# Interleaving the first expert's products with the second expert's search, two more clock-holding matmuls, and other PSUM banks for the last attention unit

## Chip, cores and metric

One NeuronCore of a Trainium2 chip. The metric is the device time of one execution in microseconds (us). All of a run's executions are listed with their mean granted TensorE clock (1 is full speed). With one core there is no second die to compare with, so a run counts as slow only if it is more than 1.5% above the fastest one of its kernel.

Engines: PE is TensorE, PEld its weight loads, DVE VectorE, ACT ScalarE, POOL GpSimd, SP the engine that issues most transfers. L1310 is a line of the kernel.

## Reference

Two blocks. A linear attention (RWKV-5) over 4 batches, 8 heads, 768 steps, and behind it a balanced mixture of 8 experts, in which each of 3072 tokens goes to one expert and each expert takes 384 of them:

```python
logits = x @ w_gate                       # x: (3072, 384), the attention's output
order = np.argsort(-logits.flatten())     # greedy: best (token, expert) pairs first
for idx in order:
    tok, e = int(idx) // E, int(idx) % E
    if assigned[tok] >= 0 or counts[e] >= cap:
        continue
    assigned[tok] = e; counts[e] += 1
...
for e in range(E):
    mask = assigned == e
    h = np.maximum(x[mask] @ w1[e], 0.0)  # 384 x 1024
    out[mask] = h @ w2[e]                 # 1024 x 384
```

## The kernel before

The kernel doesn't sort. It finds which expert fills up first and at which logit (the "search": three rounds of counting tokens above 16 thresholds), lists that expert's tokens, gathers their rows, computes that expert, strikes them out, and goes on. While TensorE computes one expert, VectorE searches for the next. A count of the search is three small matmuls, then VectorE, then one matmul that sums; a hook `between` lets other TensorE work stand between these.

```python
class Assignment:
    MEANWHILE = 2, 3, 5
    between = staticmethod(lambda n: None)
    behind = None

    def count(self, pool, m, prop, cand, digit_of):
        ...
        self.asked = tt(ind, self.by_token(m, ND), self.by_expert(cand), ALU.is_ge)   # DVE
        ...
        for j in range(NT // G):
            nc.tensor.matmul(each..., ind[...], prop[...], ...)                       # "counts", x3
        self.between(self.MEANWHILE[0])
        ...                                                                           # DVE: own, cnt, wide
        nc.tensor.matmul(all_ps..., self.ones_h, wide..., start=True, stop=True)      # the sum
        self.between(self.MEANWHILE[1])
        return all_ps

    def likely(self, fmax, acc, place, flag):
        ...
        for g in range(3):
            with ExitStack() as order:
                if self.behind is not None:
                    order.enter_context(self.tc.issue_after(self.behind))   # search behind this product
                    self.behind = None
                all_ps = self.count(pool, m, prop, cand, self.digit_of)
            ...

    def settle(self, out, ask, fetch, asked=False):
        fetch(out["tok"])                    # three indirect gathers of 128 rows
        if not asked:
            ask(out["fmax"])                 # weights of that expert
        ...
        with self.tc.If(found < 1):          # a rare path, a branch on every engine
            ...
        self.leave(out["fmax"], out["acc"])
```

The last unit of the attention and its logits (`y_ps` is one tile for all units; `turned` holds x):

```python
    def from_state(n):
        ...
                nc.tensor.matmul(y_ps[halves[i], j, g, :], state[b][heads[j], a, :], ...)
    def outputs(n):
        ...
        nc.scalar.copy(turned[n].rearrange("p (g j) t -> p j g t", j=2), y_ps[:, :, 0:2, :])
    def logits(c):
        ...
        for a in range(HP):
            for b in range(B):               # the four batches in four 32-partition strips
                nc.tensor.matmul(lg_ps[ts(b, 32), 0, :], wg_sb[:, a, :], xTs[b][:, a, :], ...)
```

The first expert's opening and the loop over experts:

```python
    def opening(hid, at):
        xT = xpool.tile([128, KD, CAP], F32, name="xT")
        h_pss = [...]                        # four PSUM tiles, one for each of four hidden columns
        turn_rows(xT, at["xg"], 0)           # transposes of the first 128 gathered rows, copied by ACT
        for c in range(NC):
            for j, h_ps in enumerate(h_pss):
                product = products(h_ps, j, at["w1"], xT, ts(c, 128))   # three 128-column matmuls
                if j == 1 and c + 1 < NC:
                    with tc.issue_after(product):
                        copied = turn_rows(xT, at["xg"], c + 1)
                    ...
        walk.behind = product                # the next search behind ALL of them
        ...

    awake = ps_t.tile([128, KD, 128], F32, name="xT_ps")
    for _ in range(4):                       # "warming": keeps TensorE busy while the rows come
        nc.tensor.matmul(awake, ident, ident.unsqueeze(1).to_broadcast([128, KD, 128]), start=True, stop=True)
    walk.settle(ahead, ask_half, fetch(xg), asked=True)
    for n in range(E):
        ...
        if n == 0:
            xT = opening(hid, at)
            done = KF // 2
        else:
            walk.behind = hidden(hid, 0, at["w1"], xT)
        if n + 1 < E:
            ahead = following(n + 2 == E)    # search, settle, weights of the next expert
        for j in range(done, KF):
            hidden(hid, j, at["w1"], xT)
        for c in range(NC):
            if c == NC - 1 and n + 1 < E:
                xT = turn(ahead["xg"])
            result(n, c, hid, at["w2"], at["tok"])
```

## Time and profile before

| | before |
|---|---|
| median of 3 runs | 425.59 us (424.44 to 425.62) |
| profiled run, its span | 425.35 us, 423.6 us |
| first products of the first expert | 142.02 us |
| first count of the second expert's search | 152.46 us |
| second expert's list ready | 167.88 us |
| TensorE waits for the second expert's rows | 4.67 us, to 176.73 us |
| first products of the second expert | 184.74 us |
| from there to the end | 238.9 us |

### The profile page before, as it was taken

What the parts mean: (1) busy time and instruction counts of PE and PEld (TensorE: products, weight loads), DVE (VectorE), ACT (ScalarE), POOL (GpSimd) and SP (SyncE); (2) the same over time, 40 slices, a digit from 0 to 9 for tenths busy, and PEclk for the clock granted to TensorE, in tenths of its full rate; (3) what the DMA queues carried; (4) which work ended last, traced back from release to release, by engine and by line L of the source; (5) the groups of instructions that cost most, each with busy time, mean ns of one, the idle gap of its engine ahead of it and who ended that gap; (6) DMA issues with size and microseconds to landing.
All of it is one profiled execution on the core that took longest, in us unless ns stands there. A gap on an engine that the chain in (4) does not pass through costs nothing. (4 is left out here: it accounts for less than half of the span.)

```text
span 423.6 us, 7986 instructions
## 1 busy us (share of the span) xinstructions
PE 401.4 (95%) x2978; PEld 266.5 (63%) x2978; DVE 198.4 (47%) x656; ACT 153.6 (36%) x390; POOL 113.4 (27%) x154
## 2 busy tenths in 40 slices
PE   7899999999987899599999999999999999999993
PEld 4688888888775775355565565565555555565551
DVE  5898889997565247127318407505704703000000
ACT  3897877878564031112022122112121221211200
POOL 5566775466001101300310310210220030211011
PEclk9999999999999899899999999999999999999999
DMA  9999999910068353702810820740550496201001
GB/s 148 164 164 188 173 179 157 185 22 4 2 215 306 86 203 135 259 19 61 313 37 7 305 82 19 235 158 19 171 221 20 149 350 207 60 19 39 0 19 37
DMA packets 93994, 54.39 MB, mean 128 GB/s; under 512 B 76785, under 2 KB 88177, under 8 KB 93937
## 3 DMA queue, kind: packets, MB, share of 16 engines
q1 hardware_dynamic: 89280, 41.70, 40.0%
q0 software_dynamic: 3072, 9.44, 6.4%
q10 hardware_dynamic: 1584, 2.56, 1.8%
q8 instruction: 27, 0.44, 0.4%
q14 instruction: 31, 0.25, 0.2%
HBM read 44.25 MB, written 9.44 MB: 127 GB/s over the span
## 5 line engine op out<-in xcount | busy, mean ns | idle before, releaser
L1289 PE MATMUL h_ps<-xT,w 128*128 128x384 f32 (+1 forms) x396 | 130.5, 479 | 0.7 <-DVE low L952 0.7
L1323 PE MATMUL o_ps<-w,hid 128*128 128x384 f32 x384 | 130.4, 491 | 0.7
L1323 PEld LDWEIGHTS o_ps<-w,hid 128*128 128x128 f32 x384 | 71.1, 191 | 47.4 <-issue 3.9
L1289 PEld LDWEIGHTS h_ps<-xT,w 128*128 128x128 f32 x396 | 69.8, 193 | 39.7 <-issue 3.8
L1296 ACT ACTIVATE hid<-h_ps 128x384 f32<-128x384 f32 x60 | 29.5, 492 | 94.0 <-PE h_ps L1289 84.2
L1326 POOL DMA_INDIRECT out_dram<-o_sb,tok x24 | 23.6, 985 | 142.3 <-ACT o_sb L1325 114.3
L453 ACT ACTIVATE AT<-ident,dd 128x128 f32<-128x128 f32 x192 | 59.6, 396 | 1.5 <-DVE dd L448 1.5
L1219 POOL DMA_INDIRECT xg<-x_rows,tok x24 | 23.6, 982 | 124.6 <-issue 101.2
L1325 ACT COPY o_sb<-o_ps 128x384 f32<-128x384 f32 x24 | 11.5, 480 | 111.5 <-PE o_ps L1323 111.5
L871 DVE TENSOR_TENSOR own<-counts,same 128x64 f32<-128x64 f32 x21 | 4.7, 225 | 89.6 <-PE counts L883 89.6
L522 DVE COPY_PREDICATED AT<-mask,g_ps 128x512 f32<-128x512 uint8 x48 | 32.5, 730 | 7.1 <-PE g_ps L520 7.1
L520 PE MATMUL g_ps<-rT,kT 48*128 48x128 f32 x384 | 28.4, 285 | 0.1
L445 POOL TENSOR_TENSOR rk<-rk,u_bc 128x384 f32<-128x384 f32 x24 | 27.3, 1135 | 1.9
L444 POOL TENSOR_TENSOR rk<-rt,kt 128x384 f32<-128x384 f32 x24 | 24.8, 1034 | 8.2 <-DMA rt<-in_r_dram 3.7
L520 PEld LDWEIGHTS g_ps<-rT,kT 48*128 48x128 f32 x384 | 23.6, 187 | 4.9 <-issue 2.9
L555 PE MATMUL y_ps<-AT,vt 128*64 128x128 f32 x384 | 25.7, 276 | 0.0
L555 PEld LDWEIGHTS y_ps<-AT,vt 128*64 128x64 f32 x384 | 20.6, 137 | 1.1 <-issue 0.3
L1279 ACT COPY xT<-xT_ps 128x384 f32<-128x384 f32 x24 | 11.0, 485 | 24.1 <-PE xT_ps L1278 14.8
L434 DVE TENSOR_TENSOR ks<-kt,wk 128x384 f32<-128x384 f32 x24 | 19.4, 808 | 0.0
L465 DVE TENSOR_TENSOR rT<-rT_ps,wr 128x512 f32<-128x512 f32 x24 | 16.4, 684 | 5.3 <-PE rT_ps L460 5.2
L1278 PE MATMUL xT_ps<-ident,xg 128*128 128x128 f32 x72 | 12.1, 294 | 5.8 <-DMA xg<-x_rows,tok 5.8
L473 ACT COPY kT<-kT_ps 128x512 f32<-128x512 f32 x24 | 14.1, 586 | 8.9 <-PE kT_ps L471 8.6
(203 smaller groups left out, 404.1 us busy)
## 6 DMA issues: line engine op xcount, KB each, us to landing
w<-in_moe_w_dram SPq DMA_DIRECT2D x14, 1536.0 KB, 10.5
kt<-in_k_dram SPq DMA_DIRECT2D x24, 192.0 KB, 4.5
rt<-in_r_dram SPq DMA_DIRECT2D x24, 192.0 KB, 5.1
vt<-in_v_dram SPq DMA_DIRECT2D x24, 192.0 KB, 4.8
x_rows<-AT SPq DMA_DIRECT2D x8, 192.0 KB, 2.7
w<-in_moe_w_dram ACTq DMA_DIRECT2D x1, 1536.0 KB
x_rows<-rt SPq DMA_DIRECT2D x6, 192.0 KB, 1.9
x_rows<-ks SPq DMA_DIRECT2D x5, 192.0 KB, 2.2
```

Source lines behind the costliest of these rows:

```text
L434: self.tc.nc.vector.tensor_mul(self.live[n]["ks"][:, :, 0:D], self.live[n]["kt"], self.wk.rearrange("p (h d) -> p h d", h=H))
L444: nc.gpsimd.tensor_mul(rk, rt[:, :, 0:D], kt)
L445: nc.gpsimd.tensor_mul(rk, rk, self.u_bc.rearrange("p (h d) -> p h d", h=H))
L453: self.tc.nc.scalar.activation(AT[:, h % 2, h // 2, :], self.ident, AF.Copy, scale=dd[:, h:h + 1])
L520: nc.tensor.matmul(g_pss[q][:, a, :], kT[heads[q], a, :], rT[heads[q], a, :], start=True, stop=True)
L522: nc.vector.copy_predicated(out=AT[:, q], mask=mask.unsqueeze(1).to_broadcast([128, HP, T]), data=g_pss[q])
L555: nc.tensor.matmul(y_ps[halves[i], j, g, :], vt[:, 2 * a + j, :], AT[:, j, a, :], start=(c == 0 and g == 0), stop=(g == 1), skip_group_che ...
L1219: nc.gpsimd.indirect_dma_start(out=xg[:, c, :], out_offset=None, in_=x_dram, in_offset=bass.IndirectOffsetOnAxis(ap=tok[:, c:c + 1], axis=0))
L1289: product = nc.tensor.matmul(h_ps[:, cols], w1[:, f, ts(j, 128)], xT[:, f, cols], start=(f == 0), stop=(f == KD - 1))
L1296: nc.scalar.activation(hid[:, j, :], h_ps, AF.Relu)
L1323: nc.tensor.matmul(o_ps, hid[:, j, ts(c, 128)], w2[:, j, :], start=(j == 0), stop=(j == KF - 1))
L1326: nc.gpsimd.indirect_dma_start(out=out_rows[n * NC + c], out_offset=bass.IndirectOffsetOnAxis(ap=tok[:, c:c + 1], axis=0), in_=o_sb, in_of ...
```

## The change

The intent: (1) the last unit writes its y to two other PSUM banks, so that it need not wait for the copy of the unit before; (2) one more warming matmul ahead of the first expert's transposes and one behind them, so that the clock stays full; (3) the opening becomes a generator, and the search for the second expert pulls its pieces through `between`, so the search runs inside the first expert's products instead of behind them.

```diff
+    def banks_of(n):
+        if n < N - 1:
+            return [y_ps[:, j] for j in range(2)]
+        if not last:
+            last.extend(mild.ps.tile([128, HP, T], F32, name=f"y_{tag}", tag=tag) for tag in ("kT_ps", "rT_ps"))
+        return last
 ...
-        nc.scalar.copy(turned[n].rearrange("p (g j) t -> p j g t", j=2), y_ps[:, :, 0:2, :])
+        into = turned[n].rearrange("p (g j) t -> p j g t", j=2)
+        if n < N - 1:
+            nc.scalar.copy(into, y_ps[:, :, 0:2, :])
+        else:
+            nc.scalar.copy(into[:, 0], y[0][:, 0:2, :])
+            nc.vector.tensor_copy(into[:, 1], y[1][:, 0:2, :])
 ...
-        for a in range(HP):
-            for b in range(B):
-                nc.tensor.matmul(lg_ps[ts(b, 32), 0, :], wg_sb[:, a, :], xTs[b][:, a, :], ...)
+        for some in ((range(B),) if c < C - 1 else (range(B - 1), (B - 1,))):
+            for a in range(HP):
+                for b in some:
+                    nc.tensor.matmul(lg_ps[ts(b, 32), 0, :], wg_sb[:, a, :], xTs[b][:, a, :], ...)
 ...
+            if pieces:
+                def between(most):
+                    for _ in range(most):
+                        next(pieces, None)
+                with tc.manual_schedule(engines={nc.tensor.engine}):
+                    next(pieces)
+                    walk.between = between
+                    walk.search(at)
+                    walk.between = Assignment.between
+                    for _ in pieces:
+                        pass
 ...
-    def opening(hid, at):
+    def opening(hid, at, xT):
         turn_rows(xT, at["xg"], 0)
+        nc.tensor.matmul(ps_t.tile([128, KD, 128], F32, name="xT_ps"), ident,
+                         ident.unsqueeze(1).to_broadcast([128, KD, 128]), start=True, stop=True)
 ...
-        walk.behind = product
+                if c > 0 or j > 1:
+                    yield
+        for j in range(len(h_pss), KF):
+            h_ps = ps_h.tile([128, CAP], F32, name="h_ps")
+            for f in range(KD):
+                nc.tensor.matmul(h_ps, at["w1"][:, f, ts(j, 128)], xT[:, f, :], ...)
+                if f < KD - 1:
+                    yield
+            nc.scalar.activation(hid[:, j, :], h_ps, AF.Relu)
+            yield
 ...
-    for _ in range(4):
+    for _ in range(5):
         nc.tensor.matmul(awake, ident, ident.unsqueeze(1).to_broadcast([128, KD, 128]), start=True, stop=True)
```

More of the change, by code (lines that the diff above doesn't have):

```diff
@@ L512, in attention_mild @@
     g_pss = [ps.tile([128, HP, T], F32, name=f"g_ps{i}") for i in range(2)]
+    last = []
     order = [(g, j, i) for g in range(2) for j in range(2) for i in range(2)]
@@ L522, in pairs @@
             nc.vector.copy_predicated(out=AT[:, q], mask=mask.unsqueeze(1).to_broadcast([128, HP, T]), data=g_pss[q])
+    def banks_of(n):
[4 more added lines that the diff above has]
+        return last
     def from_state(n):
         b, c = units[n]
+        y = banks_of(n)
         if c > 0:
@@ L528, in from_state @@
                 a = 2 * g + i
-                nc.tensor.matmul(y_ps[halves[i], j, g, :], state[b][heads[j], a, :],
+                nc.tensor.matmul(y[j][halves[i], g, :], state[b][heads[j], a, :],
                                  live[n]["rT"][heads[j], a, :], start=(g == 0), stop=False, skip_group_check=True)
@@ L552, in outputs @@
         vt, AT = (live[n][x] for x in ("vt", "AT"))
+        y = banks_of(n)
         for g, j, i in order:
             a = 2 * g + i
-            nc.tensor.matmul(y_ps[halves[i], j, g, :], vt[:, 2 * a + j, :], AT[:, j, a, :],
+            nc.tensor.matmul(y[j][halves[i], g, :], vt[:, 2 * a + j, :], AT[:, j, a, :],
                              start=(c == 0 and g == 0), stop=(g == 1), skip_group_check=True)
-        nc.scalar.copy(turned[n].rearrange("p (g j) t -> p j g t", j=2), y_ps[:, :, 0:2, :])
+        into = turned[n].rearrange("p (g j) t -> p j g t", j=2)
[4 more added lines that the diff above has]
+            nc.vector.tensor_copy(into[:, 1], y[1][:, 0:2, :])
     def logits(c):
@@ L562, in logits @@
         lg_ps = ps.tile([128, 2, 128], F32, name="lg_ps")
-        for a in range(HP):
-            for b in range(B):
-                nc.tensor.matmul(lg_ps[ts(b, 32), 0, :], wg_sb[:, a, :], xTs[b][:, a, :],
-                                 start=(a == 0), stop=(a == HP - 1), skip_group_check=True)
+        for some in ((range(B),) if c < C - 1 else (range(B - 1), (B - 1,))):
+            for a in range(HP):
+                for b in some:
+                    nc.tensor.matmul(lg_ps[ts(b, 32), 0, :], wg_sb[:, a, :], xTs[b][:, a, :],
+                                     start=(a == 0), stop=(a == HP - 1), skip_group_check=True)
         by_e = pool.tile([128, 128], F32, name="lgT")
@@ L1261, in second, with following @@
         queue.dma_start(w2, moe_w2[which(at["number"], queue)].rearrange("o (c p) d -> p (o c) d", p=128))
-    def following(last):
+    def following(last, pieces=None):
         at = dict(walk.slots(), number=xpool.tile([1, 1], I32, name="number"),
@@ L1269, in following @@
         else:
-            walk.search(at)
+            if pieces:
[9 more added lines that the diff above has]
+                        pass
+            else:
+                walk.search(at)
             walk.settle(*make)
@@ L1297, in hidden @@
         return product
-    def opening(hid, at):
-        xT = xpool.tile([128, KD, CAP], F32, name="xT")
+    def opening(hid, at, xT):
         h_pss = [pool.tile([128, CAP], F32, name=name) for pool, name in ((ps_h, "h_ps"), (ps_o, "o_ps")) for _ in range(2)]
         turn_rows(xT, at["xg"], 0)
+        nc.tensor.matmul(ps_t.tile([128, KD, 128], F32, name="xT_ps"), ident,
+                         ident.unsqueeze(1).to_broadcast([128, KD, 128]), start=True, stop=True)
         for c in range(NC):
             for j, h_ps in enumerate(h_pss):
-                product = products(h_ps, j, at["w1"], xT, ts(c, 128))
+                products(h_ps, j, at["w1"], xT, ts(c, 128))
+                if c == NC - 1:
+                    nc.scalar.activation(hid[:, j, :], h_ps, AF.Relu)
                 if j == 1 and c + 1 < NC:
-                    with tc.issue_after(product):
-                        copied = turn_rows(xT, at["xg"], c + 1)
+                    copied = turn_rows(xT, at["xg"], c + 1)
                     if c + 1 == NC - 2:
@@ L1314, in opening @@
                             second(at, nc.scalar)
-        walk.behind = product
-        for j, h_ps in enumerate(h_pss):
+                if c > 0 or j > 1:
[3 more added lines that the diff above has]
+            for f in range(KD):
+                nc.tensor.matmul(h_ps, at["w1"][:, f, ts(j, 128)], xT[:, f, :], start=(f == 0), stop=(f == KD - 1))
+                if f < KD - 1:
+                    yield
             nc.scalar.activation(hid[:, j, :], h_ps, AF.Relu)
-        return xT
+            yield
     def result(n, c, hid, w2, tok):
@@ L1337, in rwkv5_eagle_then_base_layer_balanced @@
         hid = hpool.tile([128, KF, CAP], F32, name="hid")
-        done = 1
         if n == 0:
-            xT = opening(hid, at)
-            done = KF // 2
+            xT = xpool.tile([128, KD, CAP], F32, name="xT")
+            pieces = opening(hid, at, xT)
         else:
+            pieces = None
             walk.behind = hidden(hid, 0, at["w1"], xT)
         if n + 1 < E:
-            ahead = following(n + 2 == E)
-        for j in range(done, KF):
-            hidden(hid, j, at["w1"], xT)
+            ahead = following(n + 2 == E, pieces)
+        if n > 0:
+            for j in range(1, KF):
+                hidden(hid, j, at["w1"], xT)
         for c in range(NC):
```

## The prediction

> **What bounds the kernel now.** I read the page first, then the chain of waits, then the order of time on TensorE around the places that the change touches, then busy time and granted clock in short stretches. The page's slices say that TensorE (row PE) is full nearly everywhere, and where it is not:
>
> ```profile
> PE   7899999999987899599999999999999999999993
> PEclk9999999999999899899999999999999999999999
> ```
>
> One slice is 10.6 us. PE has a dip in slices 11 to 13 (the end of the attention part and the search for the first expert) and one in slice 16, at 169 to 180 us; the granted clock dips in slice 13 and slice 16. Everywhere else PE has 9, so a microsecond won outside those dips is won nowhere, and one won in them moves everything behind them. After 180 us PE is the bound to the end: in the table by stretches it is busy 114.55 of the 115 us from 185 to 300 and 115.70 of the 116 us from 300 to 416. So the end moves by as much as the first products of the second expert move (184.74 us in the timeline).
>
> The waits of TensorE, longest first, name the gap:
>
> ```profile
> PE xT_ps L1278 <- DMA xg<-x_rows,tok: 5.8, 3, 4.7
> ...
> PE h_ps L1289 <- DVE low L952: 0.7, 1, 0.7
> ```
>
> The timeline of TensorE over the first expert (start, us, what, idle before):
>
> ```profile
> 137.03 2.82 PE L1333 MATMUL xT_ps<-ident 128*128 128x384 f32 x8 [0.73 <-PE g_ps L658]
> 140.79 0.55 PE L1278 MATMUL xT_ps<-ident,xg 128*128 128x128 f32 x3 [0.94 <-DMA xg<-x_rows,tok]
> 142.02 2.57 PE L1289 MATMUL h_ps<-xT,w 128*128 128x128 f32 x12 [0.69 <-DVE low L952]
> ...
> 151.12 1.50 PE L1289 MATMUL o_ps<-xT,w 128*128 128x128 f32 x12
> 152.46 0.25 PE L883 MATMUL counts<-prop,ind 128*128 128x64 bf16 x3
> ...
> 167.31 4.76 PE L1323 MATMUL o_ps<-w,hid 128*128 128x384 f32 x14
> 176.73 0.87 PE L1278 MATMUL xT_ps<-ident,xg 128*128 128x128 f32 x3 [4.67 <-DMA xg<-x_rows,tok]
> ```
>
> To be seen: the second expert's search starts on TensorE only at 152.46, after all of the first expert's 128-column products. VectorE had its operand long before:
>
> ```profile
> 142.63 0.55 DVE L871 TENSOR_TENSOR ind<-m,cand 128x384 bf16<-128x384 f32 x1
> ...
> 152.74 0.22 DVE L871 TENSOR_TENSOR own<-counts,same 128x64 f32<-128x64 f32 x1 [9.29 <-PE counts L883]
> ```
>
> So the search sits 9.3 us behind products that it doesn't need. Its list (tok) is done at 167.88, the gather of the rows is issued at 169.22, 170.52 and 171.78 behind an output scatter, the rows land up to 7.2 us after issue beside 3 MB of weights, and TensorE has nothing from 172.05 to 176.73. Each pause is paid twice, for the clock falls after it (columns: stretch, PE, PEld, DVE, ACT, POOL busy, granted clock, DMA share, GB/s):
>
> ```profile
> 142.00:144.00 2.00, 1.98 (x11) 1.98 (x12) 1.42 (x4) 0.00 (x0) 0.00 (x0) 0.61 0.00 0
> 144.00:146.00 2.00, 2.00 (x12) 2.00 (x12) 0.00 (x0) 0.48 (x1) 0.00 (x0) 0.54 0.00 0
> ...
> 176.00:178.00 2.00, 1.05 (x4) 0.69 (x5) 0.00 (x0) 0.36 (x1) 0.00 (x0) 0.64 0.68 248
> 178.00:180.00 2.00, 2.00 (x6) 1.29 (x6) 0.00 (x0) 0.60 (x2) 0.00 (x0) 0.50 0.08 29
> ```
>
> In quarter microseconds the clock is 0.5 from about 142.4 to 145.8 and from 176.7 to 180.0.
>
> [...]two halved stretches of 3.4 and 3.3 us, whose starts lie 34.2 us apart, ten windows. [...]the window ahead of 142.45 holds 0.82 + 0.55 + 0.43 = 1.8 us of matmuls, 53%. [...]the data of y_ps must be copied before they are overwritten; so TensorE waits for ScalarE there (0.36 us, part 1 below), and another bank removes that wait.
>
> **The change, part by part.** The order of instructions shows that nothing else moves.
>
> *1. Last unit's x in other banks.* Now the state products of the last unit start at 114.31 after a wait of 0.36 us for the copy of the unit before. With other banks they follow the matmul before them, which ends about 113.9: 0.4 us. The copy falls into two halves, ScalarE and VectorE, beside each other; by the rows (0.59 us for 512 columns, 0.48 for 384) a half of 256 takes about 0.37, 0.2 us less, but TensorE has transposes (0.66) and the other twelve logit products in that time, so that gains nothing. VectorE's small operations on the guess (0.9 us) now stand behind its half copy and still end before 118. The logits, the search (bound by VectorE from 118 to 134), the list and the gather should all come 0.4 earlier: first transposes at 140.4 instead of 140.79. **-0.4 us.**
>
> *2. Fifth warming matmul, and one more behind the first transposes.* One is two records of 0.35, 0.7 us. Five run from 136.6 to 140.15, still ahead of 140.4. The sixth lies in the 0.69 us in which TensorE waits for the copy of the first transposes (ScalarE 0.48 us plus hand-overs). Both lie in idle time, cost 0.03 us, and make the window busy to about nine tenths. Then the clock stays full: 3.4 us at half clock did 1.7 us of work. **-1.7 us.**
>
> *3. Pieces between the counts.* Work on TensorE doesn't change. A 128-column product is two records of 0.112 us (six in 1.34), a 384-column one two of 0.333 (0.667). Before, 142.02 to 172.05 is 30.03 us, less 1.7 lost to the clock: 28.3 of work. In the new order, from a first product at 141.6: six products, three transposes, three products, and the first counts at about 143.95. Their operand is ready at 143.18 - 0.4. From there, with VectorE's steps as they are measured now (counts to wide 1.13 us, summed counts to the next ind 1.8, to acc 2.04, st_ps to vals 2.94, some_ps to part 0.83):
> - sum at 145.4 (wide ready at 145.1), second counts at 147.75 (ind at 147.2), sum at 149.3 (148.9), third counts at 151.4 (151.1), sum at 152.9 (152.5), st_ps at 154.95 (acc 154.9), some_ps at 158.4 (157.9), list at 159.2 (159.2), tok at 159.8 instead of 167.88.
>
> No step waits more than a tenth; the margins are those with which the later experts run without a wait, since six 128-column products take just what two 384-column ones take. The second half of w1 and w2 are issued behind the second copy, some 2 us earlier than 145.76; the stream's first 0.79 MB at 385 GB/s should be there by 148, and is needed at 150.7.
>
> The gather now stands ahead of the scatter on GpSimd: rows asked for at 159.85, 161.1 and 162.4. With the 7.2 us of the worst landing now, the first rows are there by 167.1 and the last by 169.6. TensorE has one hidden product and fifteen output products after the list, 16 x 0.667 = 10.7 us, to about 169.9. So the gather is covered, by some 2 us for the first rows, and no pause is left. Before, from 172.05 to the next expert's products at 184.74 is 12.7 us; the same work (nine transposes and eight output products) takes an expert later 6.3 us, from 212.32 on. The difference is 4.9 us of idle time and 1.5 of half clock. **-6.4 us.**
>
> *Sum.* 0.4 + 1.7 + 6.4 = 8.5 us: second expert's first products at 176.2, and everything behind as it is. The profiled run took 425.35, which gives 416.85. I add 0.35 us for small waits and for runs in which a window still falls badly: **417.2 us**, a ratio of 1.019 to 1.020. That is just about the 2% line.
>
> **Rivals.**
> - *The pause only moves (weights instead of rows).* The second expert's w1 is asked for at about 156 now instead of 164, beside nothing, and needs some 6 us; w2 follows at 161. Both are there before 170. For it: they share the queues with the gather, which took 7.2 us to land where three transfers met. If the rows landed 10 us after issue, 1 us would come back: 418.3.
> - *The search becomes the bound.* If VectorE took longer for a step than now, TensorE would wait at each of three sums and three counts, in fixed order. Margins are 0 to 0.6 us; 0.2 at each of the eight waits is 1.6, but the gather still has 2 us to spare, and waits on TensorE add to the end directly: 418.5.
> - *The clock still falls at the start.* If [...]the window falls badly, 1.7 us come back: 418.6. Against it: 0.25 us of idle time is left in 5 us.
> - *The branch, not the gather, sets 140.79.* TensorE and VectorE go on within 0.02 us of each other there, which speaks for it. If the branch waits for the warming matmuls, the fifth costs 0.7 us: 417.6. That TensorE crosses later such branches in a row of output products without a gap speaks against it.
> - *It gains more.* The three runs before spread from 424.44 to 425.62, as the phase of the windows would do. If the new kernel loses nothing and the first part gives 0.5, 416.3.
>
> **Range and chances.** The mechanism (search earlier by 8 us, pause of 4.7 us gone) I hold for 95% sure; what is open is some tenths. 416.2 to 419.0 holds 8 in 10. The 2% line is at 417.1 against the median of before, at 416.8 against their mean; my value is just above. Chances: 0.40 faster, 0.59 within, 0.01 slower.
>
> **What the profile would show.** Step 1: last unit's state products without the wait, first transposes at 140.4. Step 2: clock 1.00 from 140 to 148, and no gap over 0.3 us between the warming matmuls and the products. Step 3: first counts at 144, tok near 160, the wait of the transposes for xg near zero, clock 1.00 from 165 to 180, second expert's first products at 176.2. Wrong, if TensorE shows waits on VectorE inside the search, if the rows land after 170, or if half clock is still there after 140.

## The result, and the profile after

The changed kernel took 417.52 us (median of 4 runs, 417.33 to 418.27), the kernel before 425.08 us (4 runs, 424.44 to 425.62). The ratio is 0.9826, 95% interval 0.9804 to 0.9848, so the sign is sure and the 2% line is inside the interval. A ratio here is the mean time of one kernel's fast runs over that of the other's of the same rounds, so not quite the ratio of the medians. (The prediction writes its ratio the other way round: its 1.019 to 1.020 is 0.980 to 0.981 here.) On a second chip the same pair gave 0.9841 (0.9814 to 0.9867), 416.87 us against 424.48 us.

Start-up differs by some tenths from run to run (a matmul near 113 us, `most_ps`, which the change doesn't touch, starts at 113.47 us in the profile before and at 112.3 to 114.1 us in the others). Below, "M+" is a time from that matmul on; it takes this noise out.

The page's slices of the profile after (busy share of TensorE and granted clock, 40 slices of 10.4 us): the dip near 170 us is gone in both rows, and only the dip of the attention's end is left.

```profile
PE   7899999999987899999999999999999999999993
PEclk9999999999999999999999999999999999999998
```

The timeline of TensorE after the change (start, us, what, idle before):

```profile
137.15 3.46 PE L1373 MATMUL xT_ps<-ident 128*128 128x384 f32 x10 [0.86 <-PE g_ps L676]
140.92 0.52 PE L1310 MATMUL xT_ps<-ident,xg 128*128 128x128 f32 x3 [0.30 <-DMA xg<-x_rows,tok]
141.27 0.81 PE L1335 MATMUL xT_ps<-ident 128*128 128x384 f32 x2
142.13 1.60 PE L1321 MATMUL h_ps<-xT,w 128*128 128x128 f32 x12
...
144.56 0.25 PE L901 MATMUL counts<-prop,ind 128*128 128x64 bf16 x3
...
159.93 0.18 PE L1176 MATMUL list_ps<-part,alike 128*128 128x12 f16 x1
...
170.76 0.82 PE L1310 MATMUL xT_ps<-ident,xg 128*128 128x128 f32 x6
...
176.90 2.10 PE L1321 MATMUL h_ps<-xT,w 128*128 128x384 f32 x6
```

The first count stands at 144.56 instead of 152.46 us, the list's matmul at 159.93 instead of 167.27 (the list itself is done at 160.54 instead of 167.88), and the second expert's transposes at 170.76 follow the matmul before them with no wait in brackets. In the page of waits, the entry that headed the list before (5.8 us, three times) is down to the one wait of the first expert:

```profile
PE xT_ps L1310 <- DMA xg<-x_rows,tok: 0.3, 1, 0.3
```

The clock in two stretches, before and then after (stretch, PE, PEld, DVE, ACT, POOL busy with counts, granted clock, DMA share, GB/s):

```profile
142.00:148.00 6.00, 5.98 (x39) 5.98 (x40) 1.42 (x4) 0.48 (x1) 0.00 (x0) 0.72 0.10 19
...
172.00:180.00 8.00, 3.12 (x10) 1.97 (x10) 0.00 (x0) 1.44 (x3) 1.72 (x2) 0.79 0.71 260
```

```profile
142.00:148.00 6.00, 5.96 (x55) 5.85 (x55) 3.56 (x13) 1.03 (x3) 0.00 (x0) 1.00 0.32 100
172.00:180.00 8.00, 8.00 (x31) 4.80 (x31) 0.80 (x4) 1.65 (x4) 1.66 (x2) 1.00 0.13 49
```

Both stretches are at full clock now. The first is busy in both kernels, yet does 39 matmul records before and 55 after (the kernel before, when its clock stays full, does 55 too: see part 2 below): busy time alone doesn't show a halved clock, the count does.

From M to the second expert's first products it is 71.27 us before (184.74 - 113.47) and 63.28 us after (176.90 - 113.62): 7.99 us. From there to the end it is 238.9 us in both. The profiled runs differ by 425.35 - 417.49 = 7.86 us; the rest is start-up noise. So the whole gain is made between 113 and 185 us.

### The profile page after: what moved, and what is told of

Same layout as the page of the kernel before. It is cut to its first block, busy times and chain, and to the rows that moved or that the text cites. A ratio compares the mean times of both kernels' runs of the same rounds, so it can differ in the third digit from the quotient of the medians.

```text
span 415.8 us, 7996 instructions
## 1 busy us (share of the span) xinstructions
PE 400.0 (96%) x2982; PEld 265.3 (64%) x2982; DVE 198.8 (48%) x657; ACT 152.9 (37%) x390; POOL 112.8 (27%) x154
## 5 line engine op out<-in xcount | busy, mean ns | idle before, releaser
L1321 PE MATMUL h_ps<-xT,w 128*128 128x384 f32 (+1 forms) x372 | 121.1, 475 | 0.0
L1321 PEld LDWEIGHTS h_ps<-xT,w 128*128 128x128 f32 x372 | 64.8, 190 | 37.1 <-issue 3.4
L1328 ACT ACTIVATE hid<-h_ps 128x384 f32<-128x384 f32 x56 | 27.5, 491 | 87.5 <-PE h_ps L1321 77.7
L566 PE MATMUL y_ps<-AT,vt 128*64 128x128 f32 x368 | 24.6, 276 | 0.0
L566 PEld LDWEIGHTS y_ps<-AT,vt 128*64 128x64 f32 x368 | 19.7, 137 | 0.9 <-issue 0.3
L460 PE MATMUL rT_ps<-ident,rt 128*128 128x128 f32 x96 | 16.1, 292 | 1.1 <-DVE rT L465 1.1
(218 smaller groups left out, 418.4 us busy)
```

The lines of the kernel that those rows point to most:

```text
L566: nc.tensor.matmul(y[j][halves[i], g, :], vt[:, 2 * a + j, :], AT[:, j, a, :], start=(c == 0 and g == 0), stop=(g == 1), skip_group_check= ...
L1321: product = nc.tensor.matmul(h_ps[:, cols], w1[:, f, ts(j, 128)], xT[:, f, cols], start=(f == 0), stop=(f == KD - 1))
L1328: nc.scalar.activation(hid[:, j, :], h_ps, AF.Relu)
```

## The experiments

Twelve experiments ran, two of them the same kernels as in the result and one a repeat; eight on one chip (runs of the kernel before beside them: 424.17 us median of 12, 422.64 to 426.59, mean 424.20) and four on another (the kernel before, one run: 422.64). In the diffs, "-" is the changed kernel.

| run | median us (range, n) | ratio to before [95%] | mean us |
|---|---|---|---|
| change again | 416.87 (416.75 to 417.91, 5) | 0.9841 [0.9814, 0.9867] | 417.17 |
| banks undone | 417.10 (416.30 to 417.68, 5) | 0.9841 [0.9815, 0.9867] | 417.08 |
| no added warming | 417.57 (415.89 to 418.90, 6) | 0.9859 [0.9832, 0.9885] | 417.65 |
| old order of the logits | 416.68 (416.01 to 417.80, 5) | 0.9823 [0.9797, 0.9849] | 416.75 |
| no pieces (parts 1 and 2 alone) | 423.98 (422.77 to 425.29, 6) | 0.9998 [0.9971, 1.0025] | 424.09 |
| pieces alone (part 3 alone) | 418.59 (416.96 to 419.62, 6) | 0.9867 [0.9837, 0.9897] | 418.37 |
| rows sooner | 417.37 (415.89 to 418.03, 5) | 0.9839 [0.9809, 0.9869] | 417.20 |

The theory: nearly all comes from part 3, by taking away the wait for the second expert's rows and the half clock behind it. Rivals: the pause only moves; the first parts carry a good share; the branch, not the gather, sets the first expert's start.

### Which part carries it

*The change once more*, as the base of the comparisons on this chip.

> The change as it is, run again so that its parts can be compared on one chip. Both theories: 417.3 to 418.0 us, ratio to before 0.980 to 0.985, clock 1.00 from 140 to 180 us in the profile, no wait of the transposes for xg at the second expert.

Measured: 416.87 us, M to second expert's products 63.25 us. It repeats.

*Part 3 taken away*: the opening and the loop as before, with parts 1 and 2 kept.

```diff
-    def following(last, pieces=None):
+    def following(last):
 ...
-            if pieces:
-                ...
+            walk.search(at)
 ...
-    def opening(hid, at, xT):
+    def opening(hid, at):
 ...
+        walk.behind = product
```

> The kernel before with the change's first and second part, but with the first expert's products all ahead of the search, as before. Theory (the pieces carry most of the gain, 6.4 us as predicted): first counts some 10 us after the first product, the transposes wait some 4.7 us for xg, the clock falls to 0.5 after that wait but not after the warming matmuls; 1 to 1.7 us faster than before, ratio 0.996 to 0.998. Rival (the clock at the start is the main thing): 3 us or more faster than before and the wait shrinks.

Measured: ratio 0.9998, no gain to be seen (the interval ends at 0.9971, so the expected 0.996 isn't in it and 0.998 is). In its timeline the wait for the rows is back:

```profile
175.64 1.58 PE L1296 MATMUL xT_ps<-ident,xg 128*128 128x128 f32 x6 [4.76 <-DMA xg<-x_rows,tok]
```

The stretches around its end (columns as above) have a low clock for longer than in the profile before:

```profile
172.00:180.00 8.00, 4.36 (x13) 3.08 (x14) 0.00 (x0) 1.44 (x3) 0.81 (x1) 0.62 0.56 205
180.00:185.00 5.00, 5.00 (x15) 2.81 (x14) 0.00 (x0) 0.44 (x1) 0.00 (x0) 0.92 0.00 0
```

The clock was full in its opening (1.00 from 142 to 148 us), as part 2 intends, but in this execution the lost clock at the pause is 8 x 0.38 + 5 x 0.08 = 3.4 us, against 8 x 0.21 = 1.7 in the profile before. Of this, half of the 1.7 us from 173.94 to 175.64 falls into the wait itself, where it costs nothing. At the list this profile is 1.4 us ahead of the profile before (M+52.36 against M+53.80), at the second expert's products 0.6 us (M+70.64 against M+71.27): more than half of what part 2 saved at 142 us was lost again at the pause. Over six runs parts 1 and 2 alone are worth 424.20 - 424.09 = 0.1 us.

*Part 3 alone*: the banks, the order of the logits and the warming matmuls as before.

```diff
-        if n < N - 1:            # banks_of and outputs
+        if n < N:
-        for some in ((range(B),) if c < C - 1 else (range(B - 1), (B - 1,))):
+        for some in (range(B),):
-        nc.tensor.matmul(ps_t.tile([128, KD, 128], F32, name="xT_ps"), ident, ...)
-    for _ in range(5):
+    for _ in range(4):
```

> The change with its first and second part both undone, the pieces alone. Theory: the wait for xg is gone, so 5.5 to 7 us faster than before, ratio 0.983 to 0.987; executions with the clock at 0.5 after the first transposes take up to 1.7 us longer, so the runs spread more than those of the change. Rival (parts add up only together, since a slow clock at the start delays the search and brings the wait back): 4 us or less faster than before.

Measured: by the means 424.20 - 418.37 = 5.8 us. Put on top of parts 1 and 2, part 3 is worth 424.09 - 417.17 = 6.9 us; the whole change 7.0 us here (7.4 on the first chip). Part 3 alone carries five sixths of it. By the means the other parts are worth more with it (1.2 us) than without it (0.1 us), but runs of one kernel spread by 1 to 4 us, so that difference isn't shown.

### Part 1: the other banks

*Banks and logits as before, the rest as changed.*

```diff
-        if n < N - 1:            # banks_of and outputs
+        if n < N:
-        for some in ((range(B),) if c < C - 1 else (range(B - 1), (B - 1,))):
+        for some in (range(B),):
```

> The change with its first part undone (last unit back in y_ps, one copy, logits in the old order). Theory: the part gives back in the logits what it gains before them, so the time stays within 0.2 us of the change, near 417.6. Rival (the part gains its 0.4 us and the 0.13 us later start of the first transposes in the profile after is chance): 0.4 us slower than the change, near 418.0.

Measured: mean 417.08 against 417.17 us. Part 1 is worth nothing that these runs show. The trace shows where the 0.4 us went. Before, the last unit waits, and its logits take 1.26 us:

```profile
114.31 0.67 PE L529 MATMUL y_ps<-rT,state 48*64 48x128 f32 x16 [0.36 <-ACT xT L557]
...
116.52 1.26 PE L565 MATMUL lg_ps<-xT,wg_sb 128*32 128x128 f32 x32
```

In the changed kernel the state products start at 114.04 us, M+0.42 instead of M+0.84, without a wait. But the logits take longer:

```profile
116.24 1.54 PE L583 MATMUL lg_ps<-xT,wg_sb 128*32 128x128 f32 x32
```

Both end at 117.78 us; M to the transpose behind them is 4.66 us before and 4.52 after. The 16 products are the same, two records each, and each record lasts 272 to 297 ns in both. What differs is their order: before, four products for four batches follow each other in four different 32-partition strips of the output; now the last batch's four all go to one strip.

*Old order of the logits, banks as changed.*

```diff
-        for some in ((range(B),) if c < C - 1 else (range(B - 1), (B - 1,))):
+        for some in (range(B),):
```

> The change with the logits of the last chunk in the old order (four column groups in turn, the last unit's fourth in each turn), the new banks kept. Theory: sixteen logit products take 1.26 us instead of 1.54, the logits are done 0.28 us earlier, and the first gather and everything behind it too: 0.2 to 0.3 us faster than the change, near 417.3. Rival (the fourth product waits for the last unit's copy just as long, or the gather is held by something else than the search): same as the change within 0.1 us.

Measured: the logits take 1.08 us, and the transpose behind them stands at M+4.10:

```profile
116.75 1.08 PE L583 MATMUL lg_ps<-xT,wg_sb 128*32 128x128 f32 x32
```

So the order alone costs 1.54 - 1.08 = 0.46 us, about what the other banks had won. The start times in the traces show how: in the old order (profile before) four records, one for each strip, start within 40 ns, and the next four 109 ns behind them; in the changed order the last batch's first record starts 0.48 us behind the first of the other three, and its last five follow each other alone, 109 ns apart. No run here has the same products without the strips, so what the strips themselves save isn't shown, only the 0.46 us of the order. Of the 0.42 us in which this version is ahead of the changed kernel at the transpose, 0.29 is left when the gather is asked for (M+22.73 against 23.02) and 0.20 at the second expert's products (M+63.08 against 63.28). The time, 416.68 us, is the lowest median of all, 0.4 us under the changed kernel by the means, less than the spread of either. It is the version to keep, but 0.4 us isn't shown by the times alone.

### Part 2: the warming matmuls

*Without the two added matmuls, the rest as changed*, run twice, the second time for one look on the other chip.

```diff
-        nc.tensor.matmul(ps_t.tile([128, KD, 128], F32, name="xT_ps"), ident,
-                         ident.unsqueeze(1).to_broadcast([128, KD, 128]), start=True, stop=True)
-    for _ in range(5):
+    for _ in range(4):
```

> The change without its two added warming matmuls (four ahead of the branch, none behind the first transposes). Theory: the first products then run with the clock at 0.5 for about 3.4 us, 1.7 us slower than the change, near 419.2, in most executions; where the windows fall well, nothing is lost, so the runs should spread by up to 1.7 us. Rival (the pieces alone keep the clock up, as the matmuls of the counts come in between): same as the change, clock 1.00 from 140 to 148.

> The changed kernel without the two added warming matmuls, once more. The first profile of it had full clock in the opening. If half clock is seen here for 3.4 us between 140 and 148 us, the added matmuls are worth up to 1.7 us in such runs and the mean gain of 0.5 us is a share of it; if full again, the pauses of the search are what loses the clock and the added matmuls are worth little. Time 416 to 419 us.

Measured: mean 417.65 us, 0.5 us above the changed kernel; the single look took 416.53 us. In both profiles the clock is 1.00 from 142 to 148 us without any help. So is it in the profile of part 3 alone. That raised the question whether the half clock of the profile before is the rule at all.

*The kernel before once more*, for one look.

> The kernel before once more, to see how often the clock falls in the opening of the first expert. Theory 'the half clock follows a pause at a chance phase of the clock's windows': in some profiles the clock is full from 140 to 148 us, in the run on record it was half for 3.4 us. If it is half here too and behind the second pause at 177 to 180 us as well, the opening loses the clock in the kernel before more often than the no-warming and pieces-alone profiles (full in both) suggest. Time 423 to 426 us.

Measured: 423.73 us. The opening is at full clock, and behind the second pause it is half:

```profile
142.00:148.00 6.00, 6.00 (x55) 6.00 (x55) 1.22 (x4) 0.96 (x2) 0.00 (x0) 1.00 0.35 120
...
172.00:180.00 8.00, 4.69 (x16) 3.20 (x17) 0.00 (x0) 1.43 (x3) 0.13 (x1) 0.79 0.46 171
```

So without the added matmuls, one of five profiles lost the clock in the opening (before: yes; before again, pieces alone, no warming twice: no); with them none of seven did. With the pause in place (a wait of 3.9 to 4.8 us), three of three lost it at 172 to 180 us; without the pause, none. M to the second expert's products is 69.89 us in this profile, 1.38 less than in the first profile of the same kernel, which is about the price of the half clock that it hadn't (at the list it is 1.66 us: M+52.14 against M+53.80).

What looks like chance is the place of the waits on a grid of time, and the traces hold it (views of `--windows` put on the edges of the halved stretches). While TensorE has work, each halved stretch lasts 3.41 us or twice that, and the starts in one execution lie whole multiples of 3.41 us apart (142.44 and 176.58 in the profile before: ten). So take the 3.41 us windows that end on such an edge. From 100 us to the window in which TensorE's work ends, in all fourteen traces, a window with 2.2 us or more of matmuls was never followed by half clock, one with 1.34 us or less always, and between 1.4 and 1.8 us both occur. In the profile before, the window from 139.03 to 142.44 holds both waits of the opening and 1.78 us of work, and the clock halves; in "before again", whose waits are nearly the same (0.65 us for the rows instead of 0.94), an edge falls at 141.23 and parts the waits, 2.62 us of work in one window and 2.87 in the next, and it stays full. "Pieces alone" had 1.72 us in its window (139.55 to 142.97) and kept the clock, with less work than the 1.78 us behind which it fell. The two added matmuls make the same window 3.07 us full in the changed kernel. A pause of 4.7 us leaves at least one window with at most 1.1 us of work wherever the edges lie (an estimate, 3.41 less half of 4.7; it was 0.00, 0.36 and 0.52 us of work in the three profiles).

The runs say the same in their spread, as a reading and not a proof. Of the twelve timed runs of the two kernels that have the pieces but not the added matmuls (no added warming, pieces alone), five lie at 418.8 to 419.6 us with a mean clock of 0.993 or 0.994, and seven at 415.9 to 418.4 us with 0.995 or 0.996. The nineteen timed runs of the kernels that have both matmuls and the pieces (first chip's four, change again, banks undone, logits' order) all lie at or below 418.27 us. One of them has 0.994 too, at 416.30 us, so the mean clock alone doesn't settle which runs lost it: it also counts a halved stretch at the very end, when TensorE has nothing left to do (in the trace of that run 4.6 us, and none between 100 and 410 us).

### Part 3: how much room the gather has

The prediction gave the second expert's rows 2 us to spare. *One GpSimd copy of 3.4 us between the list and the gather*, for one look:

```diff
+    held = opool.tile([128, 1280, NC], I32, name="held", bufs=1)
 ...
+    def late(xg):
+        def rows(tok):
+            nc.gpsimd.tensor_copy(held, tok[:, 0:NC].unsqueeze(1).to_broadcast([128, 1280, NC]))
+            fetch(xg)(held[:, 1279, :])
+        return rows
 ...
-        make = at, ask(at["number"], at["w1"]), fetch(at["xg"])
+        make = at, ask(at["number"], at["w1"]), (late if pieces else fetch)(at["xg"])
```

> The change with a long copy on GpSimd between the second expert's list and its gather (3840 elements, 3 to 5 us by the rows of GpSimd in the profile), the result unchanged. Theory: the gather has about 2 us to spare for the last rows, up to 4 for the first, so of a delay of d about d less 2 to 3 us comes back as a wait of the transposes for xg: 1 to 3 us, plus about 1 us of half clock when it is long. Rival (the gather is far from the limit): no wait.

Measured: 417.57 us, and no wait, against what was expected. The first gather is asked for at 164.45 us, M+50.66, instead of M+47.76, and the transposes start at 170.86 us, again without a wait. *Two such copies:*

```diff
+            nc.gpsimd.tensor_copy(held, held[:, 1279, :].unsqueeze(1).to_broadcast([128, 1280, NC]))
```

> The changed kernel with two GpSimd copies of 3.4 us each between the second expert's list and its gather, so the rows are asked for some 6.8 us later than in the changed kernel. One copy (3.4 us) cost nothing. If the spare time of the gather is between 3.4 and 6 us, the second expert's transposes wait 1 to 3 us for the rows, the second expert's first products start 65 to 66 us behind most_ps instead of 63.2, and the time is 418.5 to 420.5 us. If the spare time is over 6.8 us, no wait and about 417 us.

Measured: 418.87 us; the second expert's products stand at M+64.83 (expected 65 to 66). The gather is asked for at 168.78 us, behind a scatter that the scheduler put ahead of it, and the transposes wait:

```profile
160.48 11.13 PE L1372 MATMUL o_ps<-w,hid 128*128 128x384 f32 x34
172.28 0.52 PE L1319 MATMUL xT_ps<-ident,xg 128*128 128x128 f32 x3 [0.67 <-DMA xg<-x_rows,held]
173.43 0.55 PE L1319 MATMUL xT_ps<-ident,xg 128*128 128x128 f32 x3 [0.64 <-DMA xg<-x_rows,held]
```

It cost 0.67 + 0.64 = 1.3 us of waits (two output products more stood ahead of the transposes, which hid about as much again). Why is the room larger than 2 us? The landing time isn't a constant. The rows of transfers in the three profiles (issues, KB each, median us from issue to landing), first the changed kernel, then one copy, then two:

```profile
xg<-x_rows,tok POOLq DMA_INDIRECT x3, 6.8
```

```profile
xg<-x_rows,held POOLq DMA_INDIRECT x3, 4.7
```

```profile
xg<-x_rows,held POOLq DMA_INDIRECT x3, 3.0
```

The medians mix the three gathers of an expert. Asked one by one (`--tile xg` at each issue), the first rows of the changed kernel land 6.3 us after issue, at 167.7 us, 3.1 us ahead of their transposes at 170.76; the last, asked for at 163.88, land 7.2 us after, at 171.1, only 1.0 us ahead of theirs at 172.06. With one copy all are asked for about 3 us later, and the first rows land 2.1 us later (5.5 us after issue), the last 0.3 us earlier (3.9 us after issue), counted from M. By then more of the second expert's 3 MB of weights is through: in the changed kernel the transfers run at 340 to 400 GB/s from 164 to 169 us, and in the run with two copies that load has ended by 168 us, ahead of the gather. The 2 us of the prediction were about right for the gather as it stands, and wrong as a tolerance to delay: 2.9 us cost nothing, and 7.6 us (M+55.32) cost some 1.5.

### What sets the first expert's start

In the changed kernel the first expert's transposes start at M+27.30, before at M+27.32, although part 1 should have brought them forward. In the traces of all runs but the last one below, they start at M+27.0 to 27.6.

*The rows of x written sooner* (old order of the logits, four warming matmuls, and the transposes of x spread 2, 4, 2 over the first search's gaps instead of 2, 3, 5):

```diff
-            rows(most or N)
+            rows({2: 2, 3: 4, 5: 2}.get(most, N))
```

> The change with the logits in the old order, four warming matmuls ahead of the branch instead of five, and the rows of x turned and written in groups of 2 and 4 between the counts of the first search instead of 2 and 3, so that 2 instead of 5 are left for the end. Theory: the first gather waits for the last rows written (it is issued 2.6 us after its list is done, in all traces), so it goes out about 1 us sooner after the last unit, and the first transposes too, until the branch holds them: 0.5 to 0.9 us faster than the change, about 0.982 times 0.998 of before. Rival (the gather is held by something else, or TensorE's extra rows delay the counts): same as the run with the logits in the old order.

Measured: 417.37 us, no gain by the mean. The first gather is asked for 0.87 us sooner (M+22.15), but the transposes start at M+27.17. With its rows used up, TensorE is idle for 1.87 us in the first search, and the clock is half from 132.60 us for 3.41 us (0.87 in the stretch from 134 to 142 us), behind a window with 1.34 us of work. Three of its five timed runs have a mean clock of 0.990 to 0.992 and take 417.37 to 418.03 us, the other two 0.995 and take 415.89 and 416.83, so the lost clock may hide a small gain:

```profile
132.09 0.31 PE L1166 MATMUL some_ps<-vals,row 128*128 128x48 f16 x6 [1.87 <-DVE vals L889]
```

Asking sooner didn't bring the rows sooner: they land 5.0 us after issue in this run, at 140.74 us (M+27.15), against 3.9 us and M+26.92 in the changed kernel; no row shows why it took longer. *The first transposes without the gather*: they take the identity instead of the gathered rows (the result is wrong), four warming matmuls.

```diff
-        turn_rows(xT, at["xg"], 0)
+        xT_ps = ps_t.tile([128, KD, 128], F32, name="xT_ps")
+        for f in range(KD):
+            nc.tensor.transpose(xT_ps[:, f, :], ident, ident)
+        nc.scalar.copy(xT[:, :, ts(0, 128)], xT_ps)
```

> The changed kernel, but the first expert's first three transposes take the identity instead of the gathered rows, so that nothing on TensorE waits for the first gather; four warming matmuls. The result is wrong on purpose. Theory 'the gather sets 140.79' (that of the prediction): with nothing to wait for, the first products start clearly sooner, 0.5 us or more ahead of the 28.5 us behind the guess's most_ps matmul that they have in the changed kernel. Rival 'the branch sets it': they start no more than 0.3 us sooner than the moment at which the transposes stand in the changed kernel (27.0 to 27.3 us behind most_ps), since the branch ends no sooner; the products would then stand at about 27.0 to 27.5 us behind most_ps.

Measured: 416.83 us, and neither number came. The scheduler put the transposes ahead of the branch, they ran at M+26.33, and still the first products stand at M+28.40, against M+28.51 in the changed kernel:

```profile
139.44 0.49 PE L1336 MATMUL xT_ps<-ident 128*128 128x128 f32 x3
139.77 0.81 PE L1338 MATMUL xT_ps<-ident 128*128 128x384 f32 x2
141.51 1.58 PE L1321 MATMUL h_ps<-xT,w 128*128 128x128 f32 x12 [0.93 <-DVE m L966]
```

Their xT was copied by 140.57 us and TensorE's first record behind the branch is at 140.6 us; the releaser that the profile names is no input of theirs. So taking the gather away brings the products forward by 0.1 us only. But the edit also moved the branch: with the transposes and the second warming matmul ahead of it, TensorE comes past it only at 140.6 us, M+27.5. What takes the 0.9 us from there to the products stays open; it isn't the first half of w1, for from 138.5 to 143 us no packet of the weights' queue is left in this trace.

The traces do say what sets the start where nothing is taken away. TensorE's semaphore record at the branch follows the end of its last matmul ahead of the branch within 0.1 us in all fourteen traces, so a fifth warming matmul moves it back. Before, four end at 139.85 us; in the changed kernel five end at 140.61 (L920 before is L938 after):

```profile
L920 PEldq EVENT_SEMAPHORE  x1: 51/51/51, 139.9 to 139.9; - x1
```

```profile
L938 PEldq EVENT_SEMAPHORE  x1: 51/51/51, 140.7 to 140.7; - x1
```

The first rows land at 140.70 us before, and the transposes start 0.09 us behind them: there the gather sets the start. In the changed kernel the rows land at 140.54, 0.3 us earlier when counted from M, but the transposes start at 140.92, 0.2 us behind the semaphore record: there the branch sets it, and the fifth warming matmul has taken up what part 1 had won, in this profile. In its repeat the rows landed later, at M+27.18, and the transposes start 0.05 us behind them, so there the gather sets the start again. Of the eleven traces that show the landing, eight start within 0.1 us of it and three (the changed kernel's first profile, no pieces, one copy), all with five warming matmuls, start later, 0.2 to 0.3 us behind the semaphore record.

## Why the prediction was right, point by point

**The bound and the total: right.** The end moved with the second expert's first products and with nothing else. Predicted 417.2 us, measured 417.52; predicted 8.5 us for the sum less 0.35 for small things, measured 7.86 in the profiles.

**Step 1 (-0.4 us): the wait went, the gain didn't come.** The state products lost their wait as predicted. The step that failed is its last sentence, that logits, search, list and gather "should all come 0.4 earlier". The prediction had the order of the logit products in view only as work that fills the time of the copy; that four in one strip take 0.46 us longer it didn't see. Measured at the transpose behind the logits: 0.14 us, and in the times: nothing. And what reached the gather didn't reach the first transposes, as in that profile the fifth warming matmul held them (M+27.32 before, M+27.30 after).

**Step 2 (-1.7 us): right in the profiled pair, mis-sized in the mean.** The added matmuls cost nothing against before (first products at M+28.55 before, M+28.51 after), though in this profile they took up the gain of step 1, and the clock stayed full. One term of it was the price if the clock falls, and that is right: 1.66 us at the list between the two profiles of the kernel before, 1.38 at the second expert's products. But the 1.7 us are lost only in some executions: one of five profiles without them. Their mean worth is 424.20 - 424.09 = 0.1 us with part 1 while the pause is there, 0.5 us in the changed kernel against its own version without them, and at most 1.2 us with part 1 included (418.37 - 417.17); the first two are within the spread of the runs. The prediction took the profiled execution for all of them.

**Step 3 (-6.4 us): right.** From the first products on, predicted and measured: first count +2.35 and +2.43, first sum +3.8 and +3.94, second count +6.15 and +6.39, third count +9.8 and +9.99, list +17.6 and +17.80, second expert's products +34.6 and +34.77. No wait of TensorE stands inside the search. The runs give 5.8 us alone, 6.9 us on top of the other two; the two profiles of full clock in the opening, before again and after, differ by 69.89 - 63.28 = 6.6 us.

**Why the sum held although two terms were too large.** In the recorded pair, steps 2 and 3 are 1.7 + 6.4 = 8.1, and 7.99 was measured; step 1's 0.4 was the excess, and the 0.35 of safety covered it. That the two are nearly the same is luck, if of small size. On the other chip the gain is 7.0 us. There, five of the twelve runs of the kernel before have a mean clock of 0.991 and take 423.2 us in the mean, the other seven have 0.984 to 0.989 and take 424.9. I read the 1.7 us between them as one halved stretch more, so that step 2 has nothing to win in some of these runs; the runs without a trace don't say where the stretch lies, and the end of the span, halved at no cost for 1.3 us in one profile of that kernel and for 4.3 us in the other, is in these means too.

**Rivals.** "The pause only moves": no; the first rows come 3.1 us ahead of need and the last 1.0, and all may be asked for 2.9 us later at no cost. "The search becomes the bound": no, the margins held. "The clock still falls at the start": not in any of seven profiles with the added matmuls. Transposes held it too: from 118 to 131.6 us of the profile after, those of x alone (L612, fp32) take 11.1 of the 13.6 us, all matmuls 11.8, and the granted clock is 1.00; where they ran out ("rows sooner", 1.34 us of work in a window), it halved. "The branch sets 140.79": no in the kernel before, where the branch record stands 0.8 us ahead of the rows; yes in the profile after, but not in its repeat. TensorE's record at the branch does follow the warming matmuls, as this rival feared (within 0.1 us of their end), but the fifth cost no 0.7 us, since TensorE had waited 0.94 us for the rows there. "It gains more": with the old order of the logits by a few tenths, within the spread.

**Its signs of being wrong.** Two stayed away: no wait of TensorE on VectorE inside the search, and no half clock from 140 us until TensorE's work ends. The third came: the last rows landed at 171.1 us, after 170. It did no harm, since their transposes stand at 172.06. A term was too short there: the gather was asked for 0.84 us behind its list (160.54 to 161.38), not 0.05; no row shows what it waited for.

**Readings that don't hold.** In the profile before, VectorE is idle for 3.28 us ahead of `fe` at 140.81 us, and the releaser named is the branch. That is no measure of a compare-and-branch, whose record there is 62 ns. In the profile after, at the branches of the first two experts, the record is 45 to 63 ns on four engines and 242 and 334 ns on TensorE. VectorE's ends at 138.1 us for the first expert, and its next one at that line comes at 140.3; for the second expert the two are at 160.8 and 161.3:

```profile
L938 DVEq COMPARE_BRANCH  x1: 63/63/63, 138.0 to 138.0; - x1
L938 DVEq EVENT_SEMAPHORE  x1: 21/21/21, 140.3 to 140.3; - x1
```

And the 2% line against the mean of before is 416.7 us, not 416.8 (0.98 x 425.22).

## What to carry to other kernels

When an operand chain (search, list, gather) of another engine hangs behind products that it doesn't need, cut those products into pieces and give the chain its turns between them: here the same work in another order was worth 6 to 7 us of 425. Before counting on a halved clock as a cost, look at several executions: one profile showed 3.4 us of it in the opening that the other four without the added matmuls hadn't. And when a wait is removed by splitting a loop, check what the new order does to the matmuls that ran beside each other (here 0.46 us lost on 16 products), and whether something else, here one more matmul ahead of a branch, takes the freed time; most of what part 1 had won went there in the profiles.
